# Seven score maxima of a fused attention and MLP kernel, moved from the first block to the first output period

## The chip, the cores and the metric

One core of a Trainium2 chip runs the whole program. The metric is the device time of one execution in microseconds (us). Five engines work side by side and wait for each other through semaphores: PE (matrix multiply), DVE (vector), ACT (activation), POOL (general vector work) and SP, which issues nearly all DMA transfers. Each takes its own instructions strictly in the order in which the program lists them.

## The reference

One transformer layer on 2048 rows of 512 numbers: a layer norm, attention with 32 heads of width 16, a residual sum, a second layer norm, and an MLP of width 1792 with SiLU, again with a residual sum.

```python
scores = jnp.einsum("bhqd,bhkd->bhqk", q, k) * scale
p = _softmax(scores, axis=-1)
o = jnp.einsum("bhqk,bhkd->bhqd", p, v)
...
h = x + _A_ref(_layernorm(x, axis=-1), A_wqkv, A_wo)
h2 = h + _B_ref(_layernorm(h, axis=-1), B_w1, B_w2)      # w2 @ silu(w1 @ x)
```

## The kernel before, in words

After the projections comes the attention. The queries are cut into four blocks of 512 rows. An **item** is one block with four heads; there are 32 items, items 0 to 7 are the first block, 8 to 15 the second, and so on. An item is cut into 16 **groups** of 128 keys each (`KC = 16`), numbered through: group g is group c = g % 16 of item i = g // 16.

One group does, on PE: four score products (one for each head, keys by queries, names `qs,ks`), a few **maxima**, and the product of probabilities and values of the group two before it (`pt,va`, eight instructions in a burst; `LAG = 2`). ACT takes the exponential of every score tile. So the burst of eight `pt,va` comes once a group, and the distance of two bursts is the time of a group.

A maximum belongs to a later item: the softmax needs the largest score of every query ahead of the exponential. `maximum` (line 291) computes 128 queries by 512 keys of scores on PE (`ks,qs`) into a PSUM bank, and DVE reduces them to one number a query (L307). An item needs 64 of them, its **piece**. When the 64th is there, `found_maxima` (line 415) starts a chain: `finish_max` (line 314) joins the partial maxima, on POOL in nine small instructions while the first block runs, and by one DVE reduction (L321) and three on POOL afterwards. `place_far` (line 350) lets SP turn the result by a transposing DMA (`mt<-ns`), one group later SP copies it into two extra rows of the item's queries (`qs<-mt`), and only then may PE compute the item's scores. In the first block the transposing DMA is put into SP's list three groups after the last maximum (`CALM + 1`), in an output period one group after it.

The number of maxima of a group is made by `maxima` (line 1432). A running account `due` says how many should have been done; outside the stages below a group does up to three, in group c = 2 of an item (`JOINT`) two, and in the first block a group may do four where `due` has reached 4. In group c = 2 DVE also copies the finished output of the item before (`pvs`). The maxima of a group take three PSUM banks in turn, so PE can be at most three ahead of DVE.

The scores of a head use 64 of the 128 rows of the array, and so does a maximum. Two such products on different halves run at the same time; `one_max` is told the half that a score product leaves free.

After item 8's first groups (c from 9 to 12) comes the **output period** of the first block: in each of four groups `output` (line 1291) projects 128 rows, by twelve products, and `interlude` (line 469) puts further maxima between the sixth and the seventh; the table `MORE` says how many for each block and group. DVE also makes the statistics of the rows there, ACT and POOL scale, add, normalize and split them, and SP turns them (`hts<-gates`). The first three maxima of an interlude use the three banks named above, further ones score banks.

From group c = 4 of item 9 (group 148) the MLP of the first block runs **beside** the attention: a group has, on each half of the array, six half products of the MLP (`beside_products`, line 1243) beside its scores and four maxima; while the number of maxima done is behind a mark that rises by four a group, it has five.

The order of work is written by the program's own loop over the groups, and what is due later is kept in an agenda (`soon`) that `tick` empties at the start of each group. Nothing reorders it afterwards.

Of the kernel before, what the change touches and what calls it, by code (L numbers as in the profile page):

```python
# [60 lines left out]
FIRSTS = 8, 16, 24  # L61
# [3 lines left out]
AHEAD = 6  # L65

JOINT = 2
MORE = (5, 4, 4, 4), (4, 4, 4, 4), (4, 4, 4, 4)
FAR = 3
CALM = 2  # L70

# [20 lines left out]
def attention_mlp_kernel(ctx: ExitStack, tc: tile.TileContext, x, wqkv, wo, w1, w2, out):  # L92
# [88 lines left out]
    def bank(kind="st", dtype=F32):  # L181
        ps = space[:, next_bank(kind), :]
        return ps if dtype == F32 else ps.bitcast(dtype)[:, :512]
# [209 lines left out]
    at = {"item": 0, "done": 0, "half": 0, "step": 0, "due": 0, "attention": False, "group": None, "ready": 0, "next": 0, "piece": 0, "blocks": True, "alone": False}  # L393
# [75 lines left out]
    def interlude(n):  # L469

        for m in range(n):
            one_max(n=None if m < 3 else next_bank("st"))

    def weave(steps, inserts):

        for k, _ in enumerate(steps):
            if k + 1 in inserts:
                inserts[k + 1]()
# [6 lines left out]
    beside = {g for m in marks for g in range(m + BEHIND, min(groups, m + BEHIND + 8 * FC))}  # L485
    fixed = {**{8 * KC * b + c: 3 + (MORE[b - 1][c - OUTPUT - 1] if OUTPUT < c <= OUTPUT + 4 else 0) for b in range(1, NB) for c in range(BEHIND, KC + BEHIND)},
             **{g: 4 for g in beside}}
# [585 lines left out]
    def project_rows(t, ps, chunks=range(DC), start=True, stop=True):  # L1073
        oh, ol = os[t]
        return product(ps, lambda c: oh[:, chunks[c], :], lambda c: ol[:, chunks[c], :],
                       lambda c: wo_h[:, chunks[c], :], lambda c: wo_l[:, chunks[c], :], len(chunks), start, stop)
# [214 lines left out]
    def output(b, n):  # L1291
# [3 lines left out]
        if n < 4:  # L1295
            ps = bank()
            weave(project_rows(n, ps), {6: lambda: interlude(MORE[b][n])})
            if 0 < n < 3:
# [133 lines left out]
    def maxima(g):  # L1432

        i, c = divmod(g, KC)
        ready = at["ready"] = min(ITEMS, i + RING - (0 if c == KC - 1 else 1)) * 64
        late_now = at["step"] in late
        if g in beside:
            at["due"] = 0
            most = 4 - late_now + (64 + 4 * (g + LEAD) > at["done"])
            return max(0, min(most, ready - at["done"]))  # L1440
        goals = [(64 * (n + 1), KC * n) for n in range(i + 1, LAST) if g >= FIRSTS[0] * KC or n <= FIRSTS[0] + 1]
        goals += [(END - 32 * (1 - a), KC * LAST + HALF * a) for a in range(2) if g >= FIRSTS[0] * KC and KC * LAST + HALF * a > g]
        rate = 0
        for n, start in goals:
            end = max(g + 1, start - (AHEAD if g >= FIRSTS[0] * KC else 3))
            rate = max(rate, (n - (before[end] - before[g]) - at["done"]) / max(1, free[end] - free[g]))
        if g in fixed or g < FIRSTS[0] * KC:
            rate = 3 if g in fixed else max(rate, 3)
        if ready < END:
            rate = min(rate, (ready - at["done"]) / (KC - 1 - c or KC))  # L1450
        at["due"] += rate
        if g < LAG:
            at["due"] = 0
            return 0
        most = 2 if late_now or c == JOINT and 0 < i <= FIRSTS[0] else 3 + (at["due"] >= 4 and i < FIRSTS[0])
        n = max(0, min(most, int(at["due"]), ready - at["done"]))
        at["due"] = min(4, at["due"] - n)
        return n
# [4 lines left out]
    for g in range(groups):  # L1463
        tick()
        i, c = divmod(g, KC)
# [41 lines left out]
        if g == 1:  # L1507
            dve("memset", pv, 0.0)
        at["group"] = g
        n = maxima(g)  # L1510

        if g in beside and next_item() == ITEMS and (at["alone"] or current and current["half"][0] == current["half"][1]):
# [73 lines left out]
```

## Time and profile before

| | |
|---|---|
| median of 3 runs | 1539.79 us (1539.65 to 1540.43) |
| profiled execution | 1539.32 us, its span 1537.5 us |
| PE busy | 1527.7 us, 99% of the span |
| DVE busy | 1361.3 us, 89% |
| ACT busy | 1238.9 us, 81% |
| POOL busy | 589.5 us, 38% |

Times in the trace count from the start of the span. Items 1 to 7 run from about 208 to 432 us, item 8 with the output period from 432 to 478 us, and item 9, in whose fifth group the MLP begins, from 478 to 520 us. In a row of the timeline stand the start, the duration of one instruction or of a run of equal ones, engine, line and operation, the tiles written and read, their count, and in brackets how long the engine had been idle before and what ended that.

### The profile page before, as it was taken

The page shows a single profiled execution, that of the slowest core. Times are in us where ns is not written, and L with a number is a line of the kernel's source. Part 1 is how long each engine was busy: PE and PEld are TensorE (multiplying, and loading weights), DVE is VectorE, ACT ScalarE, POOL GpSimd, SP SyncE. Part 2 cuts the span into 40 slices and gives each one's busy share as a digit, 9 for nine tenths or more (in the row PEclk, how much of TensorE's full clock was granted, in tenths as well). Part 3 has the DMA queues.
Part 4 walks back from the last instruction along what each step waited for, and adds up shares of the span by engine and source line. Part 5 has one row for each costly group of instructions (what it writes and reads, how often), then busy time and mean ns, then how long its engine had stood idle before and what let it go on. Part 6 is the DMA issues. An engine that isn't in the chain of part 4 may idle for free.

```text
span 1537.5 us, 30742 instructions
## 1 busy us (share of the span) xinstructions
PE 1527.7 (99%) x11408; PEld 495.3 (32%) x11408; DVE 1361.3 (89%) x2162; ACT 1238.9 (81%) x2410; POOL 589.5 (38%) x788
## 2 busy tenths in 40 slices
PE   9999999999999999999999999999999999999999
PEld 7433322222222333333322333333322333332354
DVE  7899999999999999999999999999999999993322
ACT  5555699999988899888878998888879989888632
POOL 6643453544545444411145444301154444211100
PEclk9999999999999999999999999999999999999999
DMA  6668523433333122245424112444433221335332
GB/s 220 168 171 223 149 80 92 122 94 111 112 89 98 40 63 63 82 148 152 144 59 108 44 48 60 124 129 132 141 79 95 57 63 41 100 105 170 107 91 75
DMA packets 137059, 163.33 MB, mean 106 GB/s; under 512 B 44112, under 2 KB 81040, under 8 KB 136908
## 3 DMA queue, kind: packets, MB, share of 16 engines
q1 hardware_dynamic: 132156, 152.85, 34.7%
q10 hardware_dynamic: 4752, 8.52, 2.2%
q8 instruction: 89, 1.46, 0.4%
q14 instruction: 62, 0.51, 0.1%
HBM read 126.48 MB, written 24.63 MB: 98 GB/s over the span
## 4 chain that ended last, share of the span: by engine, by line
PE 92%; DVE 3%; ACT 2%; issue 1%; DMA 1%; POOL 1%; SPq 0%; POOLq 0%; ACTq 0%
PE ps L99 91%; ACT pt L113 2%; DVE mx L305 1%; DVE mx L307 1%; PE ps L102 0%; DMA va<-in_A_wqkv_dram 0%; DMA ks<-in_A_x_dram 0%; DVE pvs L123 0%; SPq L129 0%; DVE st L123 0%; POOL rs L106 0%; POOL wv_l L106 0%; DVE ks L123 0%; DVE xtl L123 0%; ACT pvs L113 0%
## 5 line engine op out<-in xcount | busy, mean ns | idle before, releaser
L307 DVE TENSOR_REDUCE mx<-ps 128x1 f32<-128x512 f32 x1842 | 1147.2, 684 | 55.4 <-PE ps L99 11.6
L113 ACT ACTIVATE pt<-ps 128x512 f32<-128x512 f32 x2048 | 1048.3, 605 | 127.9 <-PE ps L99 125.9
L99 PE MATMUL ps<-ks,qs 48*128 48x512 f16 x2048 | 665.6, 380 | 2.6 <-DVE mx L307 1.5
L99 PE MATMUL ps<-qs,ks 64*128 64x512 f16 x2048 | 623.0, 377 | 0.6
L99 PE MATMUL ps<-pt,va 128*17 128x512 f32 x4096 | 539.0, 598 | 0.6
L99 PE MATMUL ps<-hts,w 64*128 64x512 f16 (+2 forms) x1212 | 285.0, 372 | 0.0
L99 PEld LDWEIGHTS <-ks 64*128 64x128 f16 x2048 | 173.8, 94 | 219.9 <-issue 172.5
L99 PE MATMUL ps<-w,gates 64*128 64x512 f16 (+1 forms) x938 | 230.3, 378 | 0.2 <-ACT g L113 0.2
L99 PEld LDWEIGHTS <-qs 48*128 48x128 f16 x2048 | 166.2, 94 | 67.8 <-issue 28.4
L99 PEld LDWEIGHTS <-w 64*128 64x128 f16 (+1 forms) x1212 | 101.7, 95 | 236.8 <-ACT pt L113 107.2
L106 POOL TENSOR_TENSOR ri<-rc,minus 128x16 f32<-128x16 f32 x31 | 90.8, 2929 | 198.5 <-DMA rc<-dn 198.5
L99 PEld LDWEIGHTS <-gates 64*128 64x128 f16 (+1 forms) x1082 | 88.8, 95 | 222.2 <-ACT pt L113 97.8
L99 PEld LDWEIGHTS ps<-pt,va 128*17 128x17 f32 x4096 | 68.1, 95 | 195.3 <-issue 186.5
L305 DVE TENSOR_REDUCE mx<-ps 128x2 f32<-128x1024 f32 x103 | 119.1, 1219 | 4.3 <-PE ps L99 3.5
L113 ACT ACTIVATE g<-ps,factors 128x512 f32<-128x512 f32 x80 | 54.8, 685 | 64.9 <-PE ps L99 63.3
L106 POOL TENSOR_SCALAR t<-t,factors 128x512 f32<-128x512 f32 x42 | 29.2, 696 | 181.1 <-ACT t L113 181.1
L106 POOL TENSOR_TENSOR ot<-ot,g 128x512 f32<-128x512 f32 x12 | 15.3, 1274 | 111.3 <-ACT g L113 111.3
L123 DVE SCALAR_TENSOR_TENSOR gh<-g,factors,gh 128x512 f16<-128x512 f32 x14 | 10.5, 752 | 52.1 <-ACT gh L113 52.1
L113 ACT ACTIVATE ks<-ps 128x512 f32<-128x512 f32 x30 | 17.9, 597 | 47.9 <-PE ps L99 39.8
L106 POOL TENSOR_TENSOR t<-t,g 128x512 f32<-128x512 f32 x42 | 53.7, 1280 | 3.5
L106 POOL TENSOR_TENSOR sl<-ks,sh 128x512 f16<-128x512 f32 x30 | 34.7, 1157 | 50.3 <-ACT sh L113 32.7
L106 POOL TENSOR_SCALAR nm<-nm 128x16 f32<-128x16 f32 (+1 forms) x42 | 10.9, 260 | 107.2 <-DVE nm L321 105.5
(158 smaller groups left out, 1039.8 us busy)
## 6 DMA issues: line engine op xcount, KB each, us to landing
w<-w2d SPq DMA_DIRECT2D x182, 256.0 KB
ks<-kd SPq DMA_DIRECT2D x120, 192.0 KB
w<-w1d SPq DMA_DIRECT2D x56, 256.0 KB
ks<-in_B_w_dram ACTq DMA_DIRECT2D x28, 256.0 KB
w<-in_B_w_dram SPq DMA_DIRECT2D x28, 256.0 KB
qs<-qd SPq DMA_DIRECT2D x128, 48.0 KB
kd<-sh SPq DMA_DIRECT2D x16, 256.0 KB
qd<-sh SPq DMA_DIRECT2D x16, 256.0 KB
```

Of the source, the lines that this page charges most:

```text
L99: return tc.keep_in_program_order(nc.tensor.matmul(*a, **k))
L106: tc.keep_in_program_order(getattr(nc.gpsimd, op)(*a, **k))
L113: ins = getattr(nc.scalar, fn)(*a, **k)
L123: pin(getattr(nc.vector, fn)(*a, **k))
L305: pin(nc.vector.tensor_reduce(of, space[:, n:n + 2, :], axis=AX.X, op=ALU.max))
L307: pin(nc.vector.tensor_reduce(of[:, j:j + 1], space[:, n, :], axis=AX.X, op=ALU.max))
```

## The change

```diff
 JOINT = 2
-MORE = (5, 4, 4, 4), (4, 4, 4, 4), (4, 4, 4, 4)
+MORE = (5, 5, 5, 5), (4, 4, 4, 4), (4, 4, 4, 4)
...
-        most = 2 if late_now or c == JOINT and 0 < i <= FIRSTS[0] else 3 + (at["due"] >= 4 and i < FIRSTS[0])
+        most = 2 if late_now or c == JOINT and 0 < i <= FIRSTS[0] else 3
```

No instruction is added or removed, but many stand elsewhere. Group c = 3 of items 1 to 7 had four maxima and has three: seven fewer by the end of item 7. The second to fourth group of the first output period (138, 139, 140) have five maxima in the interlude instead of four. The remaining four go to the MLP groups 150 to 153, which have five instead of four; groups 148 and 149 had five already. From group 154 on the counts are the same.

With that the pieces of items 4 to 9 are complete later: item 4's in group 37 instead of 36, item 5's in 58 instead of 57, item 6's in 80 instead of 79, item 7's in 102 instead of 100, item 8's as the first maximum of group 124 instead of the last of group 121, item 9's as the last of group 140's own three instead of the second of group 139's interlude. Item 8 begins with group 128, item 9 with group 144. What hangs on a piece moves with it on POOL and SP.

SP around the start of item 8, first as it was. `qs_105` are item 8's queries, `ks_100` and `qs_101` are loaded for item 11, `w1d` and `w2d` are stores of split MLP weights, `w<-in_A_x` the rows of x for the output period.

```order
L129 DMA w1d<-w 128x1024
L129 DMA qs_101<-qd 48x512
L129 DMA ks_100<-kd 48x2048
L355 DMA_TRANSPOSE mt<-ns_109 128x128
L129 DMA qs_101<-qd 48x512
L129 DMA qs_105<-mt 2x8x128 x2
L129 DMA ks_100<-kd 48x2048
L129 DMA w2d<-w 128x1024
L129 DMA w<-in_A_x_dram 128x512 x2
```

And now, on the same engine at the same place:

```order
L129 DMA w1d<-w 128x1024
L129 DMA qs_101<-qd 48x512
L129 DMA ks_100<-kd 48x2048
L129 DMA qs_101<-qd 48x512
L129 DMA ks_100<-kd 48x2048
L129 DMA w2d<-w 128x1024
L355 DMA_TRANSPOSE mt<-ns_109 128x128
L129 DMA qs_105<-mt 2x8x128 x2
L129 DMA w<-in_A_x_dram 128x512 x2
```

The transposing DMA and the copies into item 8's queries stand behind the store of the last split weight, ahead of which they stood. The store reads what POOL subtracts (`w<-w`, a TENSOR_TENSOR) after a cast; on POOL the nine instructions for item 8's maxima now stand right before that last cast and subtraction.

SP in the output period, around item 9's maxima (`mt<-ns_110`, `qs_107`), as one piece of the difference:

```order
 L129 DMA qs_103<-qd 48x512
 L129 DMA ks_102<-kd 48x2048
-L355 DMA_TRANSPOSE mt<-ns_110 128x128
-L129 DMA qs_103<-qd 48x512
+L129 DMA qs_103<-qd 48x512
+L129 DMA w<-w1d 128x1024
+L133 DMA_TRANSPOSE hts<-gates 128x8x128
+L355 DMA_TRANSPOSE mt<-ns_110 128x128
+L129 DMA ks_102<-kd 48x2048
 L129 DMA w<-w1d 128x1024
 L133 DMA_TRANSPOSE hts<-gates 128x8x128
 L129 DMA qs_107<-mt 2x8x128 x2
```

Item 9's copies stood behind the first `hts<-gates`, the turned rows of the output period, and now stand behind the second.

DVE in the output period, as it is now (the interludes are the runs of five; the last of them has grown together with the three of the group behind it):

```order
L307 TENSOR_REDUCE mx<-ps 128x1 x5
L1300 TENSOR_SCALAR w<-ot_1868,mv,rs 128x512
L307 TENSOR_REDUCE mx<-ps 128x1 x3
L123 BN_STATS st<-ot_1868 128x6
L123 BN_AGGR mv<-st 128x2
L307 TENSOR_REDUCE mx<-ps 128x1 x5
L1300 TENSOR_SCALAR w<-ot_1868,mv,rs 128x512
L307 TENSOR_REDUCE mx<-ps 128x1 x3
L321 TENSOR_REDUCE nm<-mx 128x16
L123 BN_STATS st<-ot_1868 128x6
L123 BN_AGGR mv<-st 128x2
L307 TENSOR_REDUCE mx<-ps 128x1 x8
```

Before, the runs were four, three, two, two, three and seven, with `nm` between the two runs of two; three reductions more stand in this stretch, and item 9's `nm` comes after six more of them.

## The prediction

> **What bounds the kernel now.** First the page: which engine fills the span, and which the chain of waits runs over.
>
> ```profile
> PE 1527.7 (99%) x11408; PEld 495.3 (32%) x11408; DVE 1361.3 (89%) x2162; ACT 1238.9 (81%) x2410; POOL 589.5 (38%) x788
> PEclk9999999999999999999999999999999999999999
> PE 92%; DVE 3%; ACT 2%; issue 1%; DMA 1%; POOL 1%; SPq 0%; POOLq 0%; ACTq 0%
> ```
>
> PE carries the end, at the full granted clock in every slice, and DVE is close behind. The change gives PE and DVE the same instructions in another order, so nothing is won or lost except where one waits for the other, or where a group is filled well or badly. I therefore read group by group: in the timeline the distance between two bursts of eight `pt,va` is the time of a group.
>
> **The first block, where seven maxima leave.** Groups c = 2 to 4 of item 5, and the same groups of item 8, which have 2, 3 and 3 maxima already now.
>
> ```profile
> 306.29 1.05 PE L99 MATMUL ps<-pt,va 128*17 128x512 f32 x8
> 308.31 1.05 PE L99 MATMUL ps<-pt,va 128*17 128x512 f32 x8
> 310.50 0.37 PE L99 MATMUL ps<-ks,qs 48*128 48x512 f16 x1 [0.15 <-DVE mx L307]
> 310.80 1.05 PE L99 MATMUL ps<-pt,va 128*17 128x512 f32 x8
> 312.82 1.05 PE L99 MATMUL ps<-pt,va 128*17 128x512 f32 x8
> ...
> 434.35 1.05 PE L99 MATMUL ps<-pt,va 128*17 128x512 f32 x8
> 436.37 1.05 PE L99 MATMUL ps<-pt,va 128*17 128x512 f32 x8
> 438.33 1.05 PE L99 MATMUL ps<-pt,va 128*17 128x512 f32 x8
> 440.29 1.05 PE L99 MATMUL ps<-pt,va 128*17 128x512 f32 x8
> ```
>
> The three groups take 2.02, 2.49 and 2.02 us in item 5 and 2.02, 1.96 and 1.96 in item 8. The fourth maximum costs 0.53 in its own group, because PE waits for a bank that DVE must empty first (the bracket), and 0.05 or 0.06 in the next. Item 8 is this part of the change already done, with the same copy on DVE ahead of it. Seven groups, 0.58 each: **minus 4.06 us**. Bounds: minus 3.7 if the small rest stays (7 x 0.53), and no more than 4.1, since 1.96 is the time of the groups around.
>
> **The MLP groups, where four arrive.** Bursts of groups 147 on; 148 and 149 have five maxima, 150 and those behind it four.
>
> ```profile
> 484.68 1.05 PE L99 MATMUL ps<-pt,va 128*17 128x512 f32 x8
> 487.77 1.05 PE L99 MATMUL ps<-pt,va 128*17 128x512 f32 x8
> 490.86 1.05 PE L99 MATMUL ps<-pt,va 128*17 128x512 f32 x8
> 496.16 1.05 PE L99 MATMUL ps<-pt,va 128*17 128x512 f32 x8
> 501.38 1.05 PE L99 MATMUL ps<-pt,va 128*17 128x512 f32 x8
> ```
>
> And one piece of the chain of waits in order of time (start, duration, what):
>
> ```profile
> 486.13 3.08 DVE mx L307 x5
> ```
>
> With five a group takes 3.09 us, and the chain shows why: five reductions in 3.08 on DVE. The two groups behind take 5.30 together and the next two 5.22. So 150 to 153 go from 5.30 + 5.22 to 4 x 3.09 = 12.36, and the slightly long pair moves on to 154 and 155, 5.30 instead of 5.22: 12.36 + 5.30 - 5.30 - 5.22 - 5.22 = **plus 1.92 us**. Bounds: 1.8 if the long pair doesn't recur, 2.5 if DVE falls further behind with each of six such groups (0.15 each).
>
> **The output period, where three arrive.** Three bursts of `pt,va` give the price on PE: the interlude of five in group 137, then that of four in 138. Then come DVE's rows at the stretch's beginning and end, and what item 9's queries hang on.
>
> ```profile
> 448.13 1.05 PE L99 MATMUL ps<-pt,va 128*17 128x512 f32 x8
> 453.73 1.05 PE L99 MATMUL ps<-pt,va 128*17 128x512 f32 x8
> 459.11 1.05 PE L99 MATMUL ps<-pt,va 128*17 128x512 f32 x8
> ```
>
> ```profile
> 452.00 5.05 DVE L307 TENSOR_REDUCE mx<-ps 128x1 f32<-128x512 f32 x8 [0.54 <-PE ps L99]
> 474.02 3.65 DVE L307 TENSOR_REDUCE mx<-ps 128x1 f32<-128x512 f32 x6
> 477.89 5.80 DVE L307 TENSOR_REDUCE mx<-ps 128x1 f32<-128x512 f32 x9 [0.22 <-PE ps L99]
> ```
>
> ```profile
> 470.89 1.27 POOL L1304 TENSOR_TENSOR ot<-g,w 128x512 f32<-128x512 f32 x1 [0.96 <-ACT g L113]
> 475.40 1.26 SPq L133 DMA_TRANSPOSE hts<-gates  x1
> 477.43 0.39 PE L99 MATMUL ps<-qs,ks 64*128 64x512 f16 x1
> ```
>
> On PE the fifth maximum costs 5.60 - 5.38 = 0.22, since four fit two by two on the halves of the array. But between 452.00 and 477.67 DVE has no gap in its rows, and PE can run only a few banks ahead: this stretch has the length of DVE's work. A reduction takes 3.65 / 6 = 0.61 there, three of them 1.83. PE alone would say 0.66 for the three, DVE says 1.83; I take DVE.
>
> Behind that waits item 9. Its copies now stand on SP behind the second `hts<-gates`, issued at 475.40. What that one is made from comes from POOL's sum of the output's last product (470.89), and so from PE's group 140: it moves by what PE has lost by then, between 0.66 and 1.83, say 1.2. In this frame: 475.40 + 1.26 (its issue) = 476.7, plus 2.3 until the copies have landed (next part), plus 1.2, is 480.2. Item 9's scores start at 477.43 and would start at 479.26 by DVE alone. So PE waits until 480.2, **plus 2.8 us** for the period in all. Bounds: 1.83 if the copies are in time; 4.3 with the latest landing (3.2) and the largest shift (1.83).
>
> **The start of item 8.** PE's group 121 and the first group of item 8 begin with the rows at 417.65 and 431.41; POOL and SP carry item 8's maxima.
>
> ```profile
> 417.65 0.39 PE L99 MATMUL ps<-qs,ks 64*128 64x512 f16 x1
> 431.41 0.09 PEld L99 LDWEIGHTS <-ks 64*128 64x128 f16 x1 [0.85 <-DMA qs<-mt]
> ```
>
> ```profile
> 420.08 0.24 POOL L106 TENSOR_TENSOR mx<-mx 128x32 f32<-128x32 f32 x1 [4.69 <-DVE mx L307]
> 422.87 1.17 POOL L106 TENSOR_TENSOR w<-w 128x512 f16<-128x512 f32 x1
> 424.78 0.61 POOL L106 CAST w<-w 128x512 f16<-128x512 f32 x1
> 425.47 1.16 POOL L106 TENSOR_TENSOR w<-w 128x512 f16<-128x512 f32 x1
> ```
>
> ```profile
> 424.06 0.34 SPq L129 DMA_DIRECT2D w1d<-w  x1
> 425.40 1.13 SPq L355 DMA_TRANSPOSE mt<-ns  x1
> 428.19 1.40 SPq L129 DMA_DIRECT2D qs<-mt  x2
> ```
>
> POOL starts on the piece at 420.08, 2.43 after group 121 begins, when that group's third maximum is reduced. The copies are issued at 428.19 and nothing waits for them: item 8's scores start on time at 431.41, 11.3 us after POOL's start. (The 0.85 ahead of that row is the burst of `pt,va`; the weight loads of every group have it.)
>
> Now the last maximum is the first of group 124, two reductions earlier within its group: POOL starts 2.43 - 2 x 0.61 = 1.21 after the group begins, and item 8's scores come four groups of 1.96, 7.84, after it. That leaves **6.6 us**. The chain needs: the nine instructions 2.79 (420.08 to 422.87, where the next begins); then, before SP may pass the weight store that is now ahead, the cast and the subtraction, 1.85 (424.78 to 426.63); the store's issue, about 0.45 (three issues fill 424.06 to 425.40); from transposing DMA to copies 2.6 (at most the 2.79 seen here with another load between; not less than its own 1.13); the copies' landing, between 1.4 (both issued) and 3.2 (the row at 431.41 found them there), 2.3 as the middle. Together 2.79 + 1.85 + 0.45 + 2.6 + 2.3 = 10.0. PE has nothing else in its list, so it stands still for 10.0 - 6.6, **plus 3.4 us**. Bounds: 2.79 + 1.85 + 0.45 + 1.13 + 1.4 = 7.6, a wait of 1.0; 2.79 + 1.85 + 0.45 + 2.79 + 3.2 = 11.1, a wait of 4.5. Items 2 to 7 are out of danger: item 7's piece is complete ten groups ahead of its start.
>
> [...]
>
> **The sum.** -4.06 + 1.92 + 2.8 + 3.4 = +4.06 us on the profiled execution's 1539.32, so 1543.4. The median of the runs is 0.47 above that execution; the forecast for the median is **1543.9 us**, slower by 0.26%. What is won in the first block is won by PE in full, and paid back at two places where the moved maxima are needed. A measurement of this kernel tells about 0.2%, 3.1 us, from no change: faster means below 1536.7, slower above 1542.9.
>
> **The rivals.** (1) The pieces are in time: neither item 8 nor item 9 waits. Then -4.06 + 1.92 + 1.83 = -0.3, 1539.5, not slower. For it speaks that nothing waits for these copies now. Against it stands the room of 6.6 us; the rival decides from the point where the chain at item 8 is shorter than that, and even the shortest sum from rows is 7.6. Chance 0.15. (2) Item 8 waits, item 9 does not, since the second turned block of rows comes earlier than I shift it: +3.1, 1542.9, right at the border. Chance 0.15. (3) PE's stop of 3.4 us slows its clock. All slices of the row above are at 9, and no stop of PE of that length stands within them, so the trace can't tell. If the clock halved for two groups, 2 x 1.96 would come on top: 1547.8. Chance 0.07. [...] (4) DVE has more slack than its unbroken rows suggest, and added maxima cost PE's own 0.22 each with no wait at all: -4.06 + 7 x 0.22 = -2.5, 1537.3, still within 0.2%. The 3.08 of five reductions speaks against it. Chance 0.03.
>
> **How the numbers follow.** The forecast has 0.60, from bounds of +0.6 (-4.06 + 1.8 + 1.83 + 1.0) to +7.6 (-3.7 + 2.5 + 4.3 + 4.5). Both ends need every term at its edge; 1541.4 to 1546.0 is the forecast's own range. To hold 8 of 10 I take in rivals (1) and (2), 1539.0 to 1546.6, which leaves out (3), (4) and the forecast's outer edges. Slower by over 0.2%: nearly all of the forecast (0.56), half of (2), all of (3), 0.70. Within 0.2%: the rest of the forecast, half of (2), nearly all of (1) and (4), 0.27. Faster: 0.03.
>
> **What would show it.** In the profile after: item lengths of 31.4 us instead of 32.0 for items 1 to 7 (the step minus 4.06 is wrong if a group of 1.96 has become longer elsewhere in the item). A weight load of item 8's first group with several us of idle time ahead of it, put down to `qs<-mt`: its length is the term 3.4. POOL's nine instructions followed by a cast and a subtraction, and only then SP's store and the transposing DMA. In the output period the same for item 9, shorter. Four more groups of 3.09 from 150 on. The forecast is wrong if the first two `qs<-mt` waits are missing; it is too low if the granted clock shows less than 9 near item 8.

## The result, and the profile after

The median of five runs is **1548.46 us** (1547.05 to 1550.36), against 1539.79 of five runs before (1539.27 to 1540.43): slower by 8.7 us, ratio 1.0057, 95% interval 1.0043 to 1.0072. The profiled execution took 1548.36 us, its span is 1546.6 instead of 1537.5.

The page of the changed kernel, its engines and the granted clock in 40 slices:

```profile
PE 1531.7 (99%) x11408; PEld 496.8 (32%) x11408; DVE 1361.0 (88%) x2162; ACT 1238.2 (80%) x2410; POOL 587.7 (38%) x788
...
PEclk9999999999999999999999999999999999999999
```

DVE, ACT and POOL have the same work as before, within 2 us. PE is busy for 4.0 us more, with the same instructions, and the slices of the clock are too coarse to say why: each is a mean over 38 us, so that 7 us at half the clock still leave 0.91, a 9. The timeline of PE around the start of item 8 says it; the first burst is that of group 127, the next ones those of 128 and 129:

```profile
426.79 1.05 PE L99 MATMUL ps<-pt,va 128*17 128x512 f32 x8
431.96 0.61 PE L99 MATMUL ps<-qs,ks 64*128 64x512 f16 x1 [4.12 <-DMA qs<-mt]
433.78 1.91 PE L99 MATMUL ps<-pt,va 128*17 128x512 f32 x8
437.44 1.05 PE L99 MATMUL ps<-pt,va 128*17 128x512 f32 x8
```

PE waits for item 8's queries, and then the same instructions take 1.6 to 1.8 times as long: 0.61 instead of 0.39 for a score product, 1.91 instead of 1.05 for the burst. Group 128 is 6.99 us long and 129 is 3.66, where 1.96 is the rule; the one behind them has 1.96 again. Stretches of 2 us of the same place (after PE, PEld, DVE, ACT and POOL come the granted clock, the share of the DMA engines and GB/s):

```profile
428.00:430.00 2.00, 0.00 (x0) 0.00 (x0) 0.16 (x1) 0.31 (x1) 0.00 (x0) 1.00 0.02 4
430.00:432.00 2.00, 0.04 (x2) 0.04 (x4) 0.00 (x0) 0.00 (x0) 0.00 (x0) 0.65 0.08 14
432.00:434.00 2.00, 2.00 (x11) 0.54 (x15) 1.36 (x3) 1.40 (x3) 0.00 (x0) 0.50 0.74 252
434.00:436.00 2.00, 2.00 (x10) 0.13 (x4) 0.53 (x1) 0.67 (x2) 0.00 (x0) 0.50 0.00 0
436.00:438.00 2.00, 2.00 (x15) 0.43 (x11) 1.71 (x3) 1.74 (x4) 0.00 (x0) 0.64 0.00 0
438.00:440.00 2.00, 2.00 (x22) 0.44 (x14) 1.62 (x4) 1.48 (x4) 0.00 (x0) 1.00 0.00 0
```

The granted clock is halved, to 0.50. If it is at either 1.00 or 0.50, a mean of 0.65 over 2 us means, as an estimate, that it fell at 430.6, 2.8 us after PE's last work ended (426.79 + 1.05 = 427.84), and a mean of 0.64 that it came back at 437.4.

POOL and SP ahead of that wait, the first of the nine instructions for item 8's maxima and what follows the nine:

```profile
421.17 0.24 POOL L106 TENSOR_TENSOR mx<-mx 128x32 f32<-128x32 f32 x1 [5.08 <-DVE mx L307]
423.93 0.61 POOL L106 CAST w<-w 128x512 f16<-128x512 f32 x1
424.62 1.16 POOL L106 TENSOR_TENSOR w<-w 128x512 f16<-128x512 f32 x1
```

```profile
425.81 0.34 SPq L129 DMA_DIRECT2D w2d<-w  x1
426.19 1.43 SPq L355 DMA_TRANSPOSE mt<-ns  x1
429.39 1.40 SPq L129 DMA_DIRECT2D qs<-mt  x2
```

In the output period, SP ahead of item 9's wait, and PE with the wait and with bursts of groups 143, 144, 148, 149 and 155:

```profile
479.74 1.26 SPq L133 DMA_TRANSPOSE hts<-gates  x1
481.10 1.42 SPq L129 DMA_DIRECT2D qs<-mt  x2
```

```profile
481.33 1.05 PE L99 MATMUL ps<-pt,va 128*17 128x512 f32 x8
483.67 0.39 PE L99 MATMUL ps<-qs,ks 64*128 64x512 f16 x1 [1.29 <-DMA qs<-mt]
484.64 1.05 PE L99 MATMUL ps<-pt,va 128*17 128x512 f32 x8
494.01 1.05 PE L99 MATMUL ps<-pt,va 128*17 128x512 f32 x8
497.10 1.05 PE L99 MATMUL ps<-pt,va 128*17 128x512 f32 x8
514.68 1.05 PE L99 MATMUL ps<-pt,va 128*17 128x512 f32 x8
```

Two bursts of the kernel before, those of groups 127 and 144:

```profile
430.43 1.05 PE L99 MATMUL ps<-pt,va 128*17 128x512 f32 x8
478.41 1.05 PE L99 MATMUL ps<-pt,va 128*17 128x512 f32 x8
```

The distance between bursts gives the account of the two profiled executions, stage by stage:

| stage | before | after | change |
|---|---|---|---|
| to the first burst | 180.45 | 180.94 | +0.49 |
| first block, to group 127 | 249.98 | 245.85 | -4.13 |
| groups 128 and 129 | 3.92 | 10.65 | +6.73 |
| groups 130 to 144, with the output period | 44.06 | 47.20 | +3.14 |
| groups 145 to 155, with the added groups of five | 28.20 | 30.04 | +1.84 |
| to the last burst | 937.14 | 938.14 | +1.00 |

The sum is +9.07; the spans differ by 9.1. Of the 6.73, the wait is 4.19: the scores would have started at 426.79 + 0.98 = 427.77, with the burst's usual 0.98, and started at 431.96. The other 2.54 are the slow groups.

### The profile page after: what moved, and what is told of

Its sections match the earlier page's. It is cut to its first block, busy times and chain, and to the rows that moved or that the text cites. A ratio compares the mean times of both kernels' runs of the same rounds, so it can differ in the third digit from the quotient of the medians.

```text
span 1546.6 us, 30742 instructions
## 1 busy us (share of the span) xinstructions
PE 1531.7 (99%) x11408; PEld 496.8 (32%) x11408; DVE 1361.0 (88%) x2162; ACT 1238.2 (80%) x2410; POOL 587.7 (38%) x788
## 4 chain that ended last, share of the span: by engine, by line
PE 90%; DVE 4%; ACT 2%; DMA 1%; POOL 1%; issue 1%; SPq 1%; POOLq 0%; DVEq 0%; ACTq 0%
PE ps L99 89%; DVE mx L307 2%; ACT pt L113 1%; DVE mx L305 1%; PE ps L102 1%; SPq L129 1%; DMA w<-w2d 0%; DMA ks<-in_A_x_dram 0%; DVE st L123 0%; POOL w L106 0%; DMA qs<-qd 0%; DMA qs<-mt 0%; DMA mt<-ns 0%; POOL wv_l L106 0%; DVE ks L123 0%
```

## The experiments

All compare with the kernel before on the same chip, whose median there was 1539.67 to 1539.83. The diffs are against the changed kernel, except where it is said.

**Is it the stop that slows PE, or something else that happens there?** Work for PE into the pause:

```diff
+        if g == FIRSTS[0] * KC:
+            ps = bank("sm")
+            for m in range(34):
+                tr(ps[:, m % 4 * P:(m % 4 + 1) * P], ident, ident)
```

> The changed kernel, with 34 transposes of the identity into a free bank put ahead of item 8's first scores, so that PE is busy for about 3.6 of the 4.2 us that it stood still there. The scores still have to wait for their queries, so the 4.2 us are lost in any case. Theory: the stop itself lowered the granted clock, and that cost 2.5 us more; then groups 128 and 129 are back at 1.96 and the time is 1548.5 - 2.5 = 1546.0, with the granted clock at 1.00 throughout. Rival: PE is slow there for another reason (the transfers that land at that time); then groups 128 and 129 stay slow and the time stays 1548.5.

Measured: 1545.08 us (1544.46 to 1546.39), ratio to before 1.0036 (1.0022 to 1.0050). PE of this run:

```profile
427.22 3.93 PE L102 MATMUL ps<-ident 128*128 128x128 f32 x34
432.16 1.05 PE L99 MATMUL ps<-pt,va 128*17 128x512 f32 x8
```

And one stretch of it, with the granted clock behind the busy time of POOL:

```profile
425.00:440.00 15.00, 14.96 (x119) 6.20 (x115) 10.44 (x18) 11.16 (x23) 1.61 (x3) 1.00 0.21 64
```

The scores still come late, by 3.97 instead of 4.19 us, but behind them all groups are at 1.96 (one at 2.02, as in the kernel before) and the granted clock is at 1.00. SP issues the same transfers in the same order there. So the slow groups were the pause's doing: 3.4 us by the medians, 2.5 in the trace of the changed kernel.

**How long a pause does it take?** The same with 9 and with 18 transposes:

```diff
-            for m in range(34):
+            for m in range(9):
```

> The changed kernel with 9 transposes of the identity ahead of item 8's first scores: about 1.0 of the 4.2 us are filled, PE stands still for some 3.2. The wait stays. [...]

```diff
-            for m in range(34):
+            for m in range(18):
```

> The changed kernel with 18 transposes of the identity ahead of item 8's first scores: about 1.9 of the 4.2 us are filled, PE stands still for some 2.3. The wait for the queries stays. In the changed kernel and in e2_early8 the clock fell about 2.8 us after PE's last work. If the length of the stop decides, 2.3 us leave the clock alone: all runs near 1545.1, as with the stop filled. If any stop of two us is enough, some runs show 0.999 and lie 1.5 to 2.5 higher, as three of the seven of e2_early8 did.

With 9: 1546.30 us (1546.01 to 1547.82), and all four runs show 0.999 as their mean clock. With 18: 1545.20 (1544.49 to 1546.39), and all six runs show 1.000. PE and the stretches of the run with 9:

```profile
427.25 1.20 PE L102 MATMUL ps<-ident 128*128 128x128 f32 x9
431.18 0.39 PE L99 MATMUL ps<-qs,ks 64*128 64x512 f16 x1 [2.73 <-DMA qs<-mt]
432.16 1.91 PE L99 MATMUL ps<-pt,va 128*17 128x512 f32 x8
```

```profile
430.00:432.00 2.00, 0.82 (x7) 0.31 (x7) 0.36 (x1) 0.40 (x1) 0.00 (x0) 1.00 0.45 99
432.00:434.00 2.00, 2.00 (x13) 0.16 (x10) 1.53 (x3) 1.67 (x4) 0.00 (x0) 0.54 0.45 166
434.00:436.00 2.00, 2.00 (x15) 0.56 (x15) 1.33 (x3) 1.36 (x3) 0.00 (x0) 0.60 0.00 0
```

And PE with 18:

```profile
427.24 2.18 PE L102 MATMUL ps<-ident 128*128 128x128 f32 x18
431.15 0.39 PE L99 MATMUL ps<-qs,ks 64*128 64x512 f16 x1 [1.73 <-DMA qs<-mt]
432.12 1.05 PE L99 MATMUL ps<-pt,va 128*17 128x512 f32 x8
```

With 9 PE stood still for 2.73 us, and the clock fell at 432.2, by the same estimate (0.54 over 432 to 434), a whole microsecond after PE had gone on. With 18 the pause was 1.73, and the burst kept its 1.05. The two pauses came out shorter than expected (3.2 and 2.3); that 2.3 us would leave the clock alone was not tried. The clock fell 3.7 us after PE's last work here (428.45 to 432.2) and 2.8 us after it in the changed kernel, so it isn't a fixed time after the pause's beginning either.

**Does the order on SP make the wait?** Item 8's transposing DMA earlier in SP's list, ahead of the store:

```diff
-            soon(WAIT + 1 if g is None else 1 if output else CALM if g > FIRSTS[0] * KC else CALM + 1, place_far, piece)
+            soon(WAIT + 1 if g is None else 1 if output or piece[0] == FIRSTS[0] else CALM if g > FIRSTS[0] * KC else CALM + 1, place_far, piece)
```

> The changed kernel, with item 8's transposing DMA put into SP's list one group after the last maximum, not three, and so ahead of the last weight store. Theory (the chain's length sets the stop, and a short stop leaves the clock alone): the transposing DMA starts when POOL's nine instructions are done, 2.2 us earlier; the stop is 4.2 - 2.2 = 2.0 us, no slow groups behind it, time 1548.5 - 2.2 - 2.5 = 1543.8. Rival (any stop of some us lowers the clock): 2.2 us earlier but the groups behind the stop still slow, 1546.3.

Measured: 1544.68 us (1543.25 to 1546.55), ratio 1.0033 (1.0022 to 1.0045). Of seven runs three show a mean clock of 0.999 and lie at 1545.7 to 1546.6, four show 1.000 and lie at 1543.3 to 1544.7. SP and PE of the profiled one, which is of the first kind:

```profile
424.49 1.14 SPq L355 DMA_TRANSPOSE mt<-ns  x1
425.67 0.57 SPq L129 DMA_DIRECT2D ks<-kd  x1
426.34 0.37 SPq L129 DMA_DIRECT2D w2d<-w  x1
428.66 1.41 SPq L129 DMA_DIRECT2D qs<-mt  x2
```

```profile
431.25 0.60 PE L99 MATMUL ps<-qs,ks 64*128 64x512 f16 x1 [2.94 <-DMA qs<-mt]
```

The transposing DMA did start 2.2 us earlier, measured from POOL's start on the piece, but it now took 4.17 us to the copies instead of 3.20, with a load and a store issued behind it, so the wait shrank by only about 1.2: the order on SP accounts for part of the wait, not for all of it. Both expectations missed in part: the pause of about 2.9 us lowered the clock in the profiled execution, and by the mean clocks and times in some of the others and not in all. A single mean of 0.999 is a weak sign, since it also turns up in runs without such a pause: one of the five with 34 transposes (at 1546.39), and five of the 51 of the experiments below, some of these among the fastest of their kernel. None of those was profiled. That all four runs with 9 transposes show it, and none of the six with 18, is the firmer sign.

**Is the loss all in item 8's start?** The same, and item 8's maxima joined on DVE:

```diff
-            finish_max(piece, g is not None and g > FIRSTS[0] * KC)
+            finish_max(piece, g is not None and (g > FIRSTS[0] * KC or piece[0] == FIRSTS[0]))
```

> As the run before, and item 8's maxima are joined by one reduction on DVE and three instructions on POOL instead of nine on POOL, about 2 us shorter. Theory: the chain then fits into the room of 6.6 us, or misses it by a few tenths; the stop and the slow groups are gone, 1548.5 - 6.7 = 1541.8 (up to 1542.3 with a rest of the stop). Rival (the loss is not in the start of item 8): 1547 to 1548.

Measured: 1542.07 us (1541.07 to 1544.56), ratio 1.0018 (1.0008 to 1.0027), as the theory had it. Nothing waits for item 8's queries, groups 128 and 129 are at 1.96. The one reduction that now stands in item 7 makes one of its groups 2.27 long, 0.31 given back. 2.4 us over the kernel before are left, so the start of item 8 carries 6.3 of the 8.7.

**What do three more reductions in the output period cost without any wait?** The kernel before, with the new table alone:

```diff
-MORE = (5, 4, 4, 4), (4, 4, 4, 4), (4, 4, 4, 4)
+MORE = (5, 5, 5, 5), (4, 4, 4, 4), (4, 4, 4, 4)
```

> The kernel before with the table of five maxima in each interlude, but with the groups of four in the first block kept; groups 148 and 149 then have four. Items 8 and 9 get their maxima as before the change, so nothing waits for queries. DVE theory: three more reductions in a stretch where DVE has no gap cost 1.8, the two MLP groups of four instead of five give back 0.9 to 1.0, so 1540.7. PE rival: the fifth maximum costs PE's 0.22 each and no more, 0.7 - 1.0, so 1539.5.

Measured: 1540.71 us (1540.32 to 1541.45), where the DVE theory had 1540.7. That it is so close is in part luck, since 0.4 us of it stand in later groups (the end of the next section); the ratio, 1.0007 (0.9997 to 1.0016), doesn't tell it from no change. The bursts of the output period do:

```profile
448.26 1.05 PE L99 MATMUL ps<-pt,va 128*17 128x512 f32 x8
...
480.18 1.05 PE L99 MATMUL ps<-pt,va 128*17 128x512 f32 x8
```

From the burst ahead of the first interlude to that of group 144 it is 31.92 us; before it was 478.41 - 448.13 = 30.28. That is 1.64 for three, 0.55 each, not PE's 0.22.

**Is item 9's wait an order on SP?** Item 8 with the quick chain (earlier transposing DMA, maxima joined on DVE), and item 9's copies right behind its transposing DMA:

```diff
-        if at["attention"]:
+        if at["attention"] and piece[0] != FIRSTS[0] + 1:
             soon(1, out)
```

> Item 8's quick chain as in e3_fast8, and item 9's copies follow its transposing DMA at once on SP, ahead of the second block of turned rows, not behind it. Theory (item 9 waits 1.3 us because its copies stand behind that block): the wait at item 9 is gone and the time is 1542.1 - 1.3 = 1540.8; the output period keeps the 1.8 that DVE needs. Rival (item 9 waits for something earlier, the reductions themselves): the wait stays, 1542.

Measured: 1540.49 us (1540.03 to 1542.16), ratio 1.0006 (0.9996 to 1.0016). The copies stand ahead of the second block of turned rows and go out at 470.31:

```profile
467.85 1.28 SPq L355 DMA_TRANSPOSE mt<-ns  x1
470.31 1.42 SPq L129 DMA_DIRECT2D qs<-mt  x2
...
473.11 1.28 SPq L133 DMA_TRANSPOSE hts<-gates  x1
```

Group 144 is at 1.96 again. With both waits gone the change is back at the time of the kernel before, no better: in this profile the first block's 4.1 us stand against 2.0 in the output period, 1.8 in the MLP groups, 0.3 for the reduction in item 7 and 0.4 in later groups.

**Can the seven maxima be put where they cost less?** Two versions with the quick chains of the last run. In the first, all seven go to MLP groups of five, every second group from 148 on:

```diff
-MORE = (5, 5, 5, 5), (4, 4, 4, 4), (4, 4, 4, 4)
+MORE = (5, 4, 4, 4), (4, 4, 4, 4), (4, 4, 4, 4)
...
-            most = 4 - late_now + (64 + 4 * (g + LEAD) > at["done"])
+            most = 4 - late_now + (64 + 4 * (g + LEAD) > at["done"] and (g % 2 == 0 or not 148 <= g < 170))
```

> No group of four in the first block, item 8's quick chain, item 9's copies at once, no further maximum in the output period; all seven go to MLP groups of five, and these are every second group from 148 on (nine of them), not one behind the other. If DVE's average load makes a group of five 3.09 long, groups in turn cost PE's 0.22 each: -4.1 + 9 x 0.22 - 1.0 (the two that were there before) = -3.1, so 1536.6. If the last maximum of such a group waits for its bank whatever comes after, each costs 0.46: -4.1 + 9 x 0.46 - 1.0 = -1.0, so 1538.7.

Measured: 1540.02 us (1539.39 to 1540.84), ratio 1.0002 (0.9992 to 1.0011). Each group of five still takes 3.09, though a group of four (2.65, later 2.61) stands behind it:

```profile
481.45 1.05 PE L99 MATMUL ps<-pt,va 128*17 128x512 f32 x8
484.54 1.05 PE L99 MATMUL ps<-pt,va 128*17 128x512 f32 x8
487.19 1.05 PE L99 MATMUL ps<-pt,va 128*17 128x512 f32 x8
```

So it isn't DVE's load over several groups that makes a group of five long, but what its own fifth maximum meets within the group. That this is the wait for one of three banks fits, but no row shows it. The time also misses the dearer of the two expectations, 1538.7, by 1.3: against the first block's gain the profile has 0.3 for the reduction in item 7, 0.2 in the output period and 0.2 more than reckoned in the groups of five, and 0.4 stand ahead of the first group, where the order is the same.

In the second, four of the seven are put off to the end, where a group without maxima was left:

```diff
-MORE = (5, 5, 5, 5), (4, 4, 4, 4), (4, 4, 4, 4)
+MORE = (5, 4, 4, 4), (4, 4, 4, 4), (4, 4, 4, 4)
...
-CALM = 2
+CALM = 1
...
-LEAD = 4
+LEAD = 3
...
-        if at["attention"]:
+        if at["attention"] and at["group"] is not None and not (at["next"] // KC in FIRSTS):
             soon(1, out)
```

> No group of four in the first block, item 8's quick chain, no further maximum in the output period, copies at once in the output periods; and the mark of the MLP groups lies four maxima lower, so that only groups 148 to 152 have five, every later piece of an MLP stretch is complete one group later, and group 492 near the end has four instead of none. The transposing DMA follows one group after the last maximum, not two. Theory (the price of a maximum is that of the place where it is done): -4.1 in the first block, three more groups of five at 0.46 are +1.4, group 492 +0.3, no wait: -2.4, so 1537.4, below both kernels. Rival (a piece that is complete one group later makes each item wait): some 20 items from 10 on wait several tenths each, 1542 or more.

Measured: 1540.35 us (1539.50 to 1542.03), ratio 1.0004 (0.9995 to 1.0013). No item waits for its queries, so the rival fell; but the 2.4 us didn't come either. In this profile group 137 is 6.71 long instead of 5.59, with PE held up there:

```profile
450.41 0.90 PE L99 MATMUL ps<-wo_h,gates 128*128 128x512 f16 x2 [0.65 <-POOL gates L106]
```

What POOL splits for the output period (`gates`) is not ready. That PE gets there nearly 4 us sooner isn't enough to explain it: it does so in the two versions before, too, where this group has 5.78 and 5.74. What differs is a transfer ahead of POOL's work: SP could issue `den<-dr` only 3.22 us after `dr<-ri` (442.13 to 445.35), where the other ten profiles have 1.41 to 1.59. Whether that belongs to the version or to this one execution is not shown. The groups around the end of item 30 and the beginning of 31 lose another 1.2 or so. None of the versions beats the kernel before by what can be measured.

## Why the prediction was right or wrong

**The direction was right, and so was the place; the size was not, and the measured 1548.5 lies outside the range** (1539.0 to 1546.6). Step by step:

- *The first block, minus 4.06.* Right: -4.13 with the rounding of bursts, and the three groups are 2.02, 1.96 and 1.96 in every item, as item 8's were before.
- *The MLP groups, plus 1.92.* Right, 1.84: six groups of 3.09 in a row. The long pair did not recur, which was the lower bound. DVE did not fall further behind with each.
- *The output period, plus 2.8.* Right in both parts, 3.14 in all: the three reductions by DVE's price (1.85 up to group 143; 1.64 in the kernel before with the new table alone), and item 9's wait behind the second block of turned rows (1.35, since group 144 took 3.31), which vanished when its copies were put ahead. The small difference to 3.14 is group 130, which had 2.02 and has 1.96.
- *The start of item 8, plus 3.4.* The wait was there and in the way described, and 4.19 long. The room was 6.60 us (421.17 to 427.77) as worked out. Of the chain, POOL's part and the store came out as forecast (2.76, 1.85 and 0.38); transposing DMA to copies took 3.20 instead of 2.6, more than the 2.79 that I had called the most, and the landing 2.57 instead of 2.3.
- *Rival (3), "PE's stop of 3.4 us slows its clock", at 0.07.* **This is the step that failed.** It is seen in the profiled execution (0.50 from 432 to 436), and the mean clock shows it in the other runs of the changed kernel as well (0.998 in four of the five, 0.999 in the fifth, which is also the fastest). It belonged into the sum: a pause that I put at 3.4 us, and at up to 4.5, came with a price that I left to a rival. That the clock would halve, and for two groups, was a supposition of mine that no row of the kernel before showed; the runs showed 0.50. A pause of 2.73 did it in the profiled run and, by the mean clock, in all four, one of about 2.9 in the profiled run and, by the mean clock, in two more of seven. The price that I set, 3.9, was too high: the low clock lasted an estimated 6.8 us, the first 1.4 of which fell into the pause, and 2.54 us were lost. Without these 2.54 the measured median would have been 1545.9, within the range; the wait itself was 0.8 longer than forecast. The sign that the prediction named for this, a digit under 9, could not show it.

By the stages the forecast terms sum to -4.13 + 6.73 + 3.14 + 1.84 = 7.58 us. The rest of the 9.07 in the profiled execution, 0.49 ahead of the first burst and 1.00 behind group 155, stands in stretches where the order of the work is the same. The 0.49 is within what executions differ by there: the ten other profiles reach the first burst at 180.39 to 181.41. Of the 1.00, 0.39 come back at the same three groups (0.11, 0.17 and 0.11, which begin near 569, 632 and 888 us in the kernel before) in all eight profiles of kernels with the new table and in none of the three with fives in group 137 alone: a cost of the change that the prediction put at nothing, whose cause stays open. The other 0.61 stand at one group near the end, with a wait for weights:

```profile
1431.18 0.38 PE L99 MATMUL ps<-w,gates 128*128 128x512 f16 x1 [0.45 <-DMA w<-w2d]
```

Several of the experiments show such waits in their profiles and others don't, and the runs of the changed kernel spread over 3.3 us, those before over 1.2. Why they spread more here stays open.

## What to carry to other kernels

Work that is moved later shortens the room of everything that is made from it; work out for each consumer the time from the last producer to the first use, with every instruction and transfer between, and compare it with the chain, not with the fact that nothing waits now. A pause of the matrix engine is to be priced with what it does to the clock: in this kernel one of 1.73 us did nothing to it and one of 2.73 lowered it, and the 4.19 us of waiting cost 6.7. Where a stretch is DVE's, as the output period is here, an added reduction cost its full 0.55 to 0.62 us though PE could take it for 0.22.

## What the runs showed of the hardware that was not expected

In three profiles the granted clock went down. By the estimate above, with the clock at either 1.00 or 0.50, it was low in the changed kernel from 430.6 to 437.4, 6.8 us; in the run with 9 transposes from 432.2 to 435.6, 3.4 us; in the one with the earlier transposing DMA 3.4 us as well, by these two stretches of it (0.55 over the first means a fall at 431.1, 0.74 over the second a return at 434.5; the two us between them have 0.50):

```profile
431.00:432.00 1.00, 0.75 (x4) 0.28 (x6) 0.08 (x1) 0.11 (x1) 0.00 (x0) 0.55 0.71 158
434.00:435.00 1.00, 1.00 (x12) 0.14 (x6) 0.00 (x0) 0.00 (x0) 0.00 (x0) 0.74 0.00 0
```

PE had stood still for 4.12 us in the first, 2.73 in the second and 2.94 in the third. What sets how long the clock stays low, and at what moment it falls, is not shown.

A transposing DMA of a tile of 128 by 128 took 2.3 to 4.2 us from its issue to that of the copies that need it: 2.32 for item 8 with its maxima joined on DVE, 2.46 in the run with item 9's copies at once (467.85 to 470.31), 3.20 in the changed kernel, 2.90 to 2.96 in the three runs with transposes, whose SP has the same order, and 4.17 in the run with the earlier transposing DMA, where a load and a store were issued behind it. Both were issued behind it in the run with 2.32, too, so what makes the difference is not shown.
